# Attention and a gated unit on one core: new delays and slack in a list scheduler, bf16 norm sums, a shift turned in f16, and eight pairs' outputs turned by TensorE

## The chip, the core and the metric

The kernel runs on one core of one Trainium2 chip. The core has TensorE (PE: matmuls, with its weight loads told apart as PEld), VectorE (DVE), ScalarE (ACT), GpSimd (POOL) and SyncE (SP), which issues all of this kernel's DMAs. Each engine works through its own queue in order; semaphores tie the queues together. The metric is the device time of one execution in microseconds, given as a median over runs. A profile is one more execution with every instruction recorded. All times below are from such runs and profiles.

## The reference

Attention over 8 batches and 8 heads of 64, with 576 pooled queries and 1152 keys, followed by a unit with a spatial gate over the joined heads.

```python
q_pool = q.reshape(B, H, S // 2, 2, D).mean(axis=3)
scores = scale * np.matmul(q_pool, k.transpose(0, 1, 3, 2))
scores = scores - np.max(scores, axis=-1, keepdims=True)
attn = np.exp(scores)
attn = attn / (np.sum(attn, axis=-1, keepdims=True) + 1e-09)
x = np.matmul(attn, v)            # heads joined: (8, 576, 512)
...
h = np.maximum(x @ w_in, 0.0)     # 512 -> 1024
u, v = h[..., :512], h[..., 512:]
v_n = (v - mean) / np.sqrt(var + 1e-06)
v_s = np.einsum('ts,bsd->btd', w_spatial, v_n) + b_spatial
out = (u * v_s) @ w_out           # float32
```

## The kernel before

**Precision.** Nearly every f32 operand is split into a head and a rest in 16 bits (hi and lo), scaled by a power of two that `scales` (L340) finds: a matmul with a matrix of ones sums squares over the partitions, and three small VectorE instructions make two factors of the exponent.

**Pairs.** Two heads make a pair: 8 batches of 4 pairs, 32 in all. For each pair:

- `prep` (L535) scales and splits q and k and copies the parts to where the matmuls want them (DMAs).
- `maxima` (L594) computes the scores a first time, heads only, in 27 blocks of 128 x 384, into a PSUM tile named `pm` (or, while no gated unit is open, alternately `pw`). VectorE reduces each block to its row maxima (`mt`, L623).
- `shift` (L631) makes of the maxima two rows of f16 that are appended to q (`X`), so that the second product comes out with the maximum subtracted already. It is called twice a pair, for 5 and for 4 groups of 128 rows. It reduces `mt` to `mx`, turns `mx` by TensorE (L639, f32), works on the turned row in PSUM (L642), writes head and rest (L645, L646) and sends them by two DMAs (L649).
- `attention` (L792) computes the scores again in 18 blocks of 128 keys x 512 queries (`main_tile`: two matmuls each, L800 and L801, into one of three banks `pss`), takes the exponential on ScalarE into `pt` (L806, eight buffers), and splits `pt` on GpSimd (L826) into a bf16 top and an f16 rest. `values` (L700) multiplies both with v (L714, L720, L725). 64 further queries of each head go by `tail_tile` and `tail_values`.
- `values` ends each head with a division into `xm`. `turn_main` (L740) then splits the pair's 128 x 512 result into head and rest (`xc`: L746 on ScalarE; L747 on VectorE for the first eight pairs, on GpSimd after) and turns both by two DMA transposes (L750) into `xg`.

The maxima of pair i+1, the preparation of pair i+2, the values of pair i+1 and the weights (in the first eight pairs, `load_weights`, L401, with its `from_double`) are woven into the attention of pair i.

**Gated units.** Two batches make a unit (`gated_unit`, L846): some 580 matmuls of up to 512 columns through the banks `pw`. The first opens after the eighth pair, and four run in all, woven into the attention of later pairs. The last runs mostly alone.

**Order.** The program is written in a plausible order, and `Order.pin` (L183) then replaces each engine's order by that of a list schedule. `cost` (L146) gives each instruction two times: how long it holds its engine and when its result is there. `edges` (L101) gives the dependences, and the order in which buffers of a ring may be begun. The loop of `pin` always takes the engine that can start earliest and, on it, the instruction that is first in the program among those that are due. The order found is fixed by dependences that hold no semaphore. For the VectorE and GpSimd instructions that take two operands from SBUF (`two_from_sbuf`, L178) the schedule keeps them from overlapping. For loads it keeps a count of the DMA queue's backlog, `wire`.

```python
                at = {n: max(due[n], wire - 1000) if n in load else due[n] for n in ns}
                t = max(free[e], min(at.values()))
                n = min(n for n in ns if at[n] <= t)
...
            if shared[n]:
                if e == "DVE":
                    if t >= held[0]:
                        t = max(t, held[1] - 130)
```

## Time and profile before

| what | value |
|---|---|
| median of 3 runs | 1229.48 us (1221.91, 1229.48, 1231.46) |
| the profiled execution | 1221.1 us, of which the recorded span is 1219.0 us |
| mean granted TensorE clock | 0.98 of full speed |
| DMA traffic | 135.09 MB, mean 111 GB/s |
| issues of the DMA transposes of `turn_main` | 64, two a pair |
| matmuls of `scales` (f32, two instructions a call) | 48 calls |

Engine rows of the profile give busy time, share of the span and a count. A group's row names line, engine, operation, tiles written and read, shapes and count, then busy time with the mean of one in ns, then the engine's idle time just before them with what ended it. A row of waits reads: the engine and line that waited, what ended the wait, total us, times, longest. A matmul's time in a row includes its passage through the array, so the pace of matmuls is read from one start to the next; the same holds for VectorE's instructions. Stages are written as windows in us from the start of the span.

### The profile page before, as it was taken

The numbers are of one execution on the slowest core, as the hardware profiler recorded it, in microseconds if no ns is written. First come the engines' busy times: TensorE is split into PE (matmuls) and PEld (weight loads), VectorE is DVE, ScalarE is ACT, GpSimd is POOL, SyncE is SP. The second block draws the span as 40 slices with busy tenths as digits, with TensorE's granted clock in tenths as the row PEclk, the third lists the DMA queues.
The fourth block names the chain that finished last, engine by engine and source line by source line (L and its number), as shares of the span: only waits on it lengthen the run. The fifth ranks groups of instructions, "written<-read, shape, count | busy, mean of one in ns | idle before, by whom it ended". The sixth has DMA issues, their size and how long they took to land.

```text
span 1219.0 us, 34011 instructions
## 1 busy us (share of the span) xinstructions
PE 1143.2 (94%) x13504; PEld 712.6 (58%) x13504; DVE 897.0 (74%) x2163; ACT 890.6 (73%) x1659; POOL 909.6 (75%) x774
## 2 busy tenths in 40 slices
PE   3888888879999999999999999999999999999998
PEld 1555555556666666666666666666665666665453
DVE  5699999997889676865679777865669866841644
ACT  4788778678977887878777887878776786754423
POOL 2769998699888897888787887888887787874000
PEclk9989899899999999999999999999999999999999
DMA  5456464346443553266433443256343421121002
GB/s 189 162 169 169 118 196 120 112 126 169 122 123 95 122 142 105 49 167 179 117 80 99 140 118 89 63 145 196 93 115 98 106 76 47 39 53 45 1 1 78
DMA packets 97151, 135.09 MB, mean 111 GB/s; under 512 B 48544, under 2 KB 56736, under 8 KB 96480
## 3 DMA queue, kind: packets, MB, share of 16 engines
q1 hardware_dynamic: 96992, 132.92, 39.7%
q8 instruction: 106, 1.74, 0.6%
q14 instruction: 53, 0.43, 0.1%
HBM read 81.20 MB, written 9.44 MB: 74 GB/s over the span
## 4 chain that ended last, share of the span: by engine, by line
PE 72%; DVE 16%; ACT 3%; issue 1%; DMA 0%; ACTq 0%; DVEq 0%
PE pss L800 8%; PE pss L801 8%; PE pm L617 7%; PE pw L988 7%; PE pw L883 6%; DVE mt L623 6%; PE pw L1031 5%; PE pw L947 5%; PE o L725 4%; PE o L714 4%; PE o L720 4%; DVE vv L372 2%; PE pss L883 1%; PE pss L988 1%; PE pss L1031 1%
## 5 line engine op out<-in xcount | busy, mean ns | idle before, releaser
L826 POOL TENSOR_TENSOR pt<-pt 128x512 f16<-128x512 f32 x576 | 643.0, 1136 | 154.5 <-ACT pt L806 152.7
L806 ACT ACTIVATE pt<-pss,esc 128x512 f32<-128x512 f32 x576 | 386.7, 686 | 166.3 <-PE pss L801 104.0
L623 DVE TENSOR_REDUCE mt<-pm 128x1 f32<-128x384 f32 x733 | 387.9, 549 | 75.2 <-PE pm L617 66.4
L800 PE MATMUL pss<-qhi,khi 128*128 128x512 f16 x576 | 221.3, 385 | 18.3 <-ACT pt L806 16.9
L801 PE MATMUL pss<-xq,klo 66*128 66x512 f16 x576 | 221.3, 387 | 0.7 <-DMA xq<-mr 0.5
L617 PE MATMUL pm<-khi,qhi 128*128 128x384 f16 x655 | 208.6, 332 | 10.4 <-DVE mt L623 5.2
L714 PE MATMUL o<-vp,pt 128*128 128x65 f16 x2304 | 171.0, 194 | 0.4
L725 PE MATMUL o<-vp,pt 128*128 128x65 f16 x2304 | 169.7, 194 | 0.6 <-POOL pt L826 0.5
L714 PEld LDWEIGHTS <-pt 128*128 128x128 bf16 x2304 | 130.1, 99 | 67.1 <-issue 5.0
L720 PE MATMUL o<-vp,pt 128*128 128x64 f16 x2304 | 168.7, 194 | 0.0
L725 PEld LDWEIGHTS <-pt 128*128 128x128 f16 x2304 | 124.0, 99 | 32.0 <-issue 4.5
L617 PEld LDWEIGHTS <-qhi 128*128 128x128 f16 x768 | 75.3, 100 | 76.5 <-issue 30.2
L720 PEld LDWEIGHTS <-pt 128*128 128x128 bf16 x2304 | 112.2, 99 | 3.3 <-issue 0.3
L883 PE MATMUL pw<-wi_h,xg 128*128 128x512 f16 x240 | 88.4, 378 | 0.0
L801 PEld LDWEIGHTS <-klo 66*128 66x128 f16 x576 | 56.6, 99 | 51.8 <-issue 27.3
L826 POOL TENSOR_TENSOR ptl<-ptl 128x1152 f16<-128x1152 f32 x32 | 74.3, 2321 | 14.4 <-ACT ptl L822 14.4
L947 PE MATMUL pw<-xg,wi_h 128*128 128x512 f16 (+1 forms) x336 | 83.4, 325 | 0.0
L822 ACT ACTIVATE ptl<-pss,esc 128x256 f32<-128x256 f32 (+1 forms) x128 | 63.7, 497 | 26.4 <-PE pss L817 26.2
L988 PE MATMUL pw<-ws_h,vv 128*128 128x512 f16 x216 | 80.6, 379 | 0.0
L1031 PE MATMUL pw<-wo_h,vv 128*128 128x512 f16 x216 | 79.0, 378 | 1.1 <-DVE vv L372 0.9
L623 DVE TENSOR_REDUCE mt<-pw 128x1 f32<-128x384 f32 x131 | 69.6, 543 | 9.3 <-PE pw L617 8.9
L800 PEld LDWEIGHTS <-khi 128*128 128x128 f16 x576 | 57.0, 99 | 26.2 <-issue 6.8
(195 smaller groups left out, 2432.0 us busy)
## 6 DMA issues: line engine op xcount, KB each, us to landing
vt<-in_v_dram SPq DMA_DIRECT2D x56, 576.0 KB
qt<-in_qT_dram SPq DMA_DIRECT2D x32, 576.0 KB
kt<-in_kT_dram SPq DMA_DIRECT2D x32, 576.0 KB
khi<-kn SPq DMA_DIRECT2D x128, 144.0 KB
out_dram<-row SPq DMA_DIRECT2D x24, 256.0 KB
qhi<-xq SPq DMA_DIRECT2D x64, 72.0 KB
klo<-klo SPq DMA_DIRECT2D x32, 144.0 KB
vv<-in_w_in_dram SPq DMA_DIRECT2D x4, 1024.0 KB
```

Source lines behind the costliest of these rows:

```text
L617: nc.tensor.matmul(pm[:, :W], lhsT=qhl[:, h, c0 : c0 + P], rhs=khh[:, h, n * NB : (n + 1) * NB, :], start=True, stop=True,)
L623: nc.vector.reduce_max(out=mt[:, t, n : n + 1], in_=pm[:, :W], axis=AX.X)
L714: nc.tensor.matmul(o[:, t], lhsT=top[:, cols], rhs=vp[:, D : D + D1], start=c == 0 and t == 0, stop=False, skip_group_check=True,)
L720: nc.tensor.matmul(o[:, t, 0:D], lhsT=top[:, cols], rhs=vp[:, 0:D], start=False, stop=False, skip_group_check=True)
L725: nc.tensor.matmul(o[:, t], lhsT=rst[:, cols], rhs=vp[:, D : D + D1], start=False, stop=c == NC - 1, skip_group_check=True,)
L800: nc.tensor.matmul(o, lhsT=khh[:, h, c, :], rhs=qhl[:, h, q], start=True, stop=False)
L801: nc.tensor.matmul(o, lhsT=KL[0:KR, h, c, :], rhs=X[0:KR, h, q], start=False, stop=True)
L806: nc.scalar.activation(pt, ps, AF.Exp, bias=0.0, scale=esc)
L826: nc.gpsimd.tensor_sub(t.bitcast(F16)[..., 0::2], t, t.bitcast(BF16)[..., 1::2])
L883: nc.tensor.matmul(ph, lhsT=xa[:, cc, c0 : c0 + P], rhs=wa[:, cc, DH:DF], start=n == 0, stop=n == 3 * NCC - 1,)
L988: nc.tensor.matmul(pv, lhsT=l, rhs=r[:, 0:MAIN], **fl)
L1031: nc.tensor.matmul(py, lhsT=ga[:, fc, c0 : c0 + P], rhs=wa[:, fc, :], start=m == 0, stop=m == end - 1)
```

## The change

The diff has four parts, shown with the lines around them cut.

**The schedule's model.** The time from one engine's result to another engine's start, a constant 54 (140 ns towards GpSimd), becomes a table with 52 as the default. A second table, `SLACK`, adds to the time at which a TensorE instruction counts as due (not to when it could start, which is kept in `there`): 2100 ns behind GpSimd, 300 behind ScalarE and VectorE, 500 behind a DMA. A VectorE instruction with two SBUF operands is not picked while GpSimd holds such an operation, if another can start. Several constants of `cost` change, a DMA transpose's issue time among them.

```diff
+    DELAY = {("PE", "Activation"): 114, ("Activation", "Pool"): 77}
+    SLACK = {("Pool", "PE"): 2100, ("Activation", "PE"): 300, ("DVE", "PE"): 300, ("SP", "PE"): 500}
...
-            return 500, 2400 + big / 230
+            return (1230 if "Transpose" in ins.opcode else 560), 2400 + big / (100 if "Transpose" in ins.opcode else 230)
...
-            t = 0.84 * n + (175 if psum else 200) + 90 * min(flat, 2)
+            t = 0.84 * n + (157 if psum else 188) + 85 * (min(flat, 2) or (n == 1 and wide > 1))
             if len(ins.outs) > 1:
-                t += 90
+                return t - 10, t + 95
+            return t - 105, t
...
-            t = {F32: 2.1, F16: 2.0, BF16: 1.74}[xs[1].dtype] * n + 190
-        return t - 80, t
+            t = {F32: 2.1, F16: 2.0, BF16: 1.74}[xs[1].dtype] * n + 150
+            return t - 42, t
+        return t - 84, t
...
                     at = {n: max(due[n], wire - 1000) if n in load else due[n] for n in ns}
+                    if e == "DVE":
+                        for n in ns:
+                            if shared[n] and max(free[e], at[n]) >= held[0]:
+                                at[n] = max(at[n], held[1] - 130)
...
             own, out = cost[n]
+            t = max(free[e], there[n])
...
-                end = wire + 1900
+                end = wire + 1700
...
                 elif lane[m] != e:
-                    x = end + (140 if lane[m] == "Pool" else 54)
+                    x = end + self.DELAY.get((e, lane[m]), 52)
                 else:
-                    x = t if e == "PE" else end
-                due[m] = max(due[m], x)
+                    x = t if e == "PE" else end + 34
+                there[m] = max(there[m], x)
+                due[m] = max(due[m], x + (self.SLACK.get((e, lane[m]), 0) if through else 0))
```

**The norm sums.** `ones` becomes bf16, and the sums of squares are read as their upper halves, so the matmul is of 16-bit operands. The sums lose their lower bits; the factors come from the exponent alone.

```diff
-    ones = const.tile([P, P], F32, name="ones")
+    ident_h = const.tile([P, P], F16, name="ident_h")
+    nc.vector.tensor_copy(out=ident_h, in_=ident)
+    ones = const.tile([P, P], BF16, name="ones")
...
-        nc.tensor.matmul(pt[:, :n], lhsT=ones, rhs=sq, start=True, stop=True)
+        nc.tensor.matmul(pt[:, :n], lhsT=ones, rhs=sq.bitcast(BF16)[:, 1::2], start=True, stop=True)
```

**The shift.** The arithmetic is done before the turn, on 128 x 5 or 128 x 4 values in the free columns of the last maxima bank, and head and rest are turned together in f16 into the same bank. One copy then takes them to SBUF. No bank of its own is taken.

```diff
-        mx = sm.tile([P, NT], F32, name="mx", bufs=2)
-        nc.vector.reduce_max(out=mx[:, :n], in_=mt[:, a:z], axis=AX.X)
-        yield
-        yield
-        pt = ps_m.tile([P, 512], F32, name="pm")
-        nc.tensor.transpose(out=pt[:n, :P], in_=mx[:, :n], identity=ident)
-        mr = sm.tile([NT, 2, P], F16, name="mr", bufs=2)
-        m = pt[:n, :P]
-        nc.vector.tensor_scalar(
-            out=m, in0=m, scalar1=st["lnp"][:n], scalar2=1.0 / MROW, op0=ALU.subtract, op1=ALU.mult
-        )
-        nc.vector.tensor_copy(out=mr[:n, 0], in_=m)
-        nc.vector.tensor_sub(mr[:n, 1], m, mr[:n, 0])
+        m = pm[:, KEYS // 3 : KEYS // 3 + n]
+        nc.vector.reduce_max(out=m, in_=mt[:, a:z], axis=AX.X)
+        nc.vector.tensor_scalar(out=m, in0=m, scalar1=st["lnp"], scalar2=1.0 / MROW, op0=ALU.subtract, op1=ALU.mult)
+        mc = sm.tile([P, 2 * NT], F16, name="mc", bufs=2)
+        nc.vector.tensor_copy(out=mc[:, 0:n], in_=m)
+        nc.vector.tensor_sub(mc[:, n : 2 * n], m, mc[:, 0:n])
+        yield
+        yield
+        t = pm.bitcast(F16)[: 2 * n, 2 * (512 - P // 2) :]
+        nc.tensor.transpose(out=t, in_=mc[:, : 2 * n], identity=ident_h)
+        mr = sm.tile([2 * NT, P], F16, name="mr", bufs=2)
+        nc.vector.tensor_copy(out=mr[: 2 * n], in_=t)
...
-            nc.sync.dma_start(out=rows[:, a * P : z * P], in_=mr[:n, r])
+            nc.sync.dma_start(out=rows[:, a * P : z * P], in_=mr[r * n : (r + 1) * n])
```

**The first eight pairs' outputs.** `EARLY` is 8, the number that stood in the code at three places. For those pairs TensorE turns `xm` itself, in f32, in four transposes into one `pm` bank, and `x_split` (L685) makes head and rest from PSUM, straight into `xg`. For the others the old way stays, as `turn_by_dma`.

```diff
+        if i < EARLY:
+            ps = ps_m.tile([P, 512], F32, name="pm")
+            for t in range(4):
+                nc.tensor.transpose(out=ps[:, t * P : (t + 1) * P], in_=xm[:, t], identity=ident)
+            m0 = 0 if e == 0 else MAIN + P
+            x_split(n, hp, slice(m0, m0 + MAIN), ps)
+        else:
+            turn_by_dma(xm, n, e, hp)
...
         xc = wk.tile([P, 2, 4, P], F16, name="xc", bufs=1)
         nc.scalar.activation(xc[:, 0], xm, AF.Copy, bias=0.0, scale=1.0)
-        (nc.vector if i < 8 else nc.gpsimd).tensor_sub(xc[:, 1], xm, xc[:, 0])
+        nc.gpsimd.tensor_sub(xc[:, 1], xm, xc[:, 0])
```

More of the change, by code (lines that the diff above doesn't have):

```diff
@@ L210, in pin @@
         due = [0.0] * len(prog)
+        there = [0.0] * len(prog)
         free = dict.fromkeys(self.LANES, 0.0)
@@ L282, in attn_sgu_kernel @@
     WS_STEPS = 2
+    EARLY = 2 * NHP
     MOE_RATE = 0.5
@@ L517, in split_v @@
             hd = vp[:, h, :, D : 2 * D]
-            if i < 8:
+            if i < EARLY:
                 head(hd, vt[:, h], s_v)
@@ L572, in prep @@
         for a, z in ((0, 5), (5, NC)):
-            if i < 8:
+            if i < EARLY:
                 head(kn[:, a:z], k0[:, a:z], s_k)
@@ L626, in maxima, with shift @@
             if t == 4:
-                yield from shift(st, mt, 0, 5)
+                yield from shift(st, mt, pm, 0, 5)
         yield
-        yield from shift(st, mt, 5, NT)
-    def shift(st, mt, a, z):
+        yield from shift(st, mt, pm, 5, NT)
+    def shift(st, mt, pm, a, z):
         X = st["X"]
         n = z - a
-        mx = sm.tile([P, NT], F32, name="mx", bufs=2)
-        nc.vector.reduce_max(out=mx[:, :n], in_=mt[:, a:z], axis=AX.X)
+        m = pm[:, KEYS // 3 : KEYS // 3 + n]
[4 more added lines that the diff above has]
+        nc.vector.tensor_sub(mc[:, n : 2 * n], m, mc[:, 0:n])
         yield
         yield
-        pt = ps_m.tile([P, 512], F32, name="pm")
-        nc.tensor.transpose(out=pt[:n, :P], in_=mx[:, :n], identity=ident)
-        mr = sm.tile([NT, 2, P], F16, name="mr", bufs=2)
-        m = pt[:n, :P]
-        nc.vector.tensor_scalar(
-            out=m, in0=m, scalar1=st["lnp"][:n], scalar2=1.0 / MROW, op0=ALU.subtract, op1=ALU.mult
-        )
-        nc.vector.tensor_copy(out=mr[:n, 0], in_=m)
-        nc.vector.tensor_sub(mr[:n, 1], m, mr[:n, 0])
+        t = pm.bitcast(F16)[: 2 * n, 2 * (512 - P // 2) :]
+        nc.tensor.transpose(out=t, in_=mc[:, : 2 * n], identity=ident_h)
+        mr = sm.tile([2 * NT, P], F16, name="mr", bufs=2)
+        nc.vector.tensor_copy(out=mr[: 2 * n], in_=t)
         for r in range(2):
             rows = X[D + r : D + r + 1].rearrange("p h s -> p (h s)")
-            nc.sync.dma_start(out=rows[:, a * P : z * P], in_=mr[:n, r])
+            nc.sync.dma_start(out=rows[:, a * P : z * P], in_=mr[r * n : (r + 1) * n])
         yield
@@ L738, in values, with turn_by_dma @@
                 later.append([2, lambda: turn_main(i)])
-    def turn_main(i):
-        b, hp = divmod(i, NHP)
-        n, e = divmod(b, 2)
-        xm = state.pop(i)["xm"]
+    def turn_by_dma(xm, n, e, hp):
         xc = wk.tile([P, 2, 4, P], F16, name="xc", bufs=1)
         nc.scalar.activation(xc[:, 0], xm, AF.Copy, bias=0.0, scale=1.0)
-        (nc.vector if i < 8 else nc.gpsimd).tensor_sub(xc[:, 1], xm, xc[:, 0])
+        nc.gpsimd.tensor_sub(xc[:, 1], xm, xc[:, 0])
         m0 = 0 if e == 0 else MAIN + P
@@ L753, in turn_main @@
             )
+    def turn_main(i):
+        b, hp = divmod(i, NHP)
+        n, e = divmod(b, 2)
+        xm = state.pop(i)["xm"]
+        if i < EARLY:
+            ps = ps_m.tile([P, 512], F32, name="pm")
[5 more added lines that the diff above has]
+            turn_by_dma(xm, n, e, hp)
         if hp == NHP - 1:
```

## The prediction

> **What bounds the kernel now.** I read the page's first lines, then the busy time by windows, the waits and the chain in the stages so found, and last the groups of the lines that the diff touches.
>
> ```profile
> span 1219.0 us, 34011 instructions
> PE 1143.2 (94%) x13504; PEld 712.6 (58%) x13504; DVE 897.0 (74%) x2163; ACT 890.6 (73%) x1659; POOL 909.6 (75%) x774
> ...
> 0.00:30.00 30.00, 10.21 (x36) 4.11 (x37) 17.34 (x42) 13.21 (x28) 7.58 (x16) 0.93 0.58 192
> 30.00:285.00 255.00, 211.82 (x2750) 138.06 (x2749) 229.54 (x501) 195.58 (x358) 213.53 (x163) 0.91 0.52 146
> 285.00:1110.00 825.00, 816.52 (x10046) 518.30 (x10044) 599.34 (x1503) 641.87 (x1200) 683.16 (x591) 1.00 0.40 108
> 1110.00:1219.00 109.00, 104.69 (x682) 52.15 (x677) 50.80 (x120) 39.90 (x76) 5.33 (x5) 0.99 0.09 30
> ```
>
> The window rows give length, then busy us of PE, PEld, DVE, ACT and POOL, then the clock. The 94% is a mean over two regimes. From 285 us on, where gated units feed TensorE, it is busy in 816.5 of 825 us at full clock: there only less TensorE work or fewer gaps count. From 30 to 285 us (the first eight pairs) TensorE has 43 us idle, VectorE 25, GpSimd 41: a loop in which VectorE is the fullest, with GpSimd behind it. Since the units wait for pair eight, a microsecond saved there is a microsecond of the end.
>
> The waits from 30 to 285 us, and three pieces of the chain:
>
> ```profile
> POOL pt L826 <- ACT pt L806: 36.4, 13, 10.2
> ACT pt L806 <- PE o L725: 31.8, 15, 5.8
> DVE pm L642 <- PE pm L639: 4.8, 4, 2.1
> ...
> 106.96 5.62 DMA xq<-mr
> 140.93 3.25 DVE mt L623 x7
> 167.46 1.10 PE pm L757 x8
> ```
>
> GpSimd starves at pair borders and ScalarE then waits for buffers. 3.25 us for seven reduces is 464 ns a piece, though each shows 549 below: VectorE's instructions overlap by some 80 ns, which I take off every VectorE duration.
>
> **The change part by part.** Groups of the touched lines:
>
> ```profile
> L639 PE MATMUL pm<-ident,mx 128*5 128x128 f32 (+1 forms) x46 | 12.5, 272 | 0.0
> L345 PE MATMUL pm<-sq,ones 128*128 128x2 f32 x44 | 7.0, 228 | 0.0
> ...
> L345 PE MATMUL pm<-vt,ones 128*128 128x1 f32 x10 | 1.4, 209 | 0.0
> ...
> L345 PE MATMUL pm<-gt,ones 128*128 128x1 f32 x6 | 0.8, 208 | 0.0
> L345 PE MATMUL pm<-wst,ones 128*128 128x1 f32 x2 | 0.3, 210 | 0.0
> ...
> L623 DVE TENSOR_REDUCE mt<-pm 128x1 f32<-128x384 f32 x733 | 387.9, 549 | 75.2 <-PE pm L617 66.4 <-PE pm L608 3.6
> L642 DVE TENSOR_SCALAR pm<-pm,lnp 5x128 f32<-5x128 f32 x64 | 22.0, 344 | 55.2 <-PE pm L639 55.0
> L646 DVE TENSOR_TENSOR mr<-pm,mr 5x128 f16<-5x128 f32 x64 | 17.5, 274 | 1.2
> L645 DVE CAST mr<-pm 5x128 f16<-5x128 f32 x64 | 17.5, 273 | 0.9
> L355 DVE TENSOR_SCALAR qkr<-pm 128x2 int32<-128x2 int32 x32 | 4.9, 154 | 0.7
> L688 DVE TENSOR_TENSOR xg<-pm,xg 128x256 f16<-128x256 f32 x8 | 3.3, 415 | 0.1
> ```
> ```profile
> 301.94 0.29 PE L725 MATMUL o<-vp,pt 128*128 128x65 f16 x4
> ...
> 302.06 0.36 PE L345 MATMUL pm<-sq,ones 128*128 128x2 f32 x2
> ...
> 302.28 0.32 PE L608 MATMUL pm<-kn,qd 128*128 128x384 f16 x1
> ...
> 374.89 0.22 PE L947 MATMUL pw<-xg,wi_h 128*128 128x128 f16 x1
> 374.94 0.27 PE L639 MATMUL pm<-ident,mx 128*5 128x128 f32 x1
> 375.05 0.33 PE L617 MATMUL pm<-khi,qhi 128*128 128x384 f16 x1
> ```
>
> The matmul groups are those of 285 to 1110 us, the VectorE groups those of the whole run.
>
> *Norm sums.* A call holds TensorE from 302.06 to 302.28, 0.22 us for two f32 passes. One 16-bit pass over two columns is nearest to L725, four from 301.94 to 302.06, 0.03 each. That saves 0.19. In the bound stage stand 44 + 10 + 6 + 2 instructions, 31 calls: 5.9 us. Earlier calls hide under VectorE.
>
> *The turn in the shift.* L639 holds TensorE for 0.11 us (374.94 to 375.05). The f16 matmul of 128 columns before it takes 0.05. 46 turns in the stage save 0.06 each: 2.8, taken as 2.5. Norm sums and turns together: 8.4 us, bounds 6 and 9. This is the sure part.
>
> *VectorE in the shift.* Now 344 + 273 + 274, each less 80: 0.65 us a call. After it: three instructions on 128 x 5, priced by L355 at 154 less 80, and one copy of 128 values a row, priced by L645 at 193: 0.42. Twice a pair saves 0.46, over eight pairs 3.7 us. VectorE still stands before its last copy until TensorE has turned; behind it are the next reduces. That wait was 4.8 us in this stage, so 0 is taken, within plus or minus 4.8. The bank now stays in use from reduce to copy, but the old form took one for the turn and its three instructions: one of two is blocked either way. Beyond 285 us the saved VectorE time is worth nothing by itself.
>
> *Outputs of eight pairs.* The rows of what goes, and of what is slowed by GpSimd:
>
> ```profile
> L747 DVE TENSOR_TENSOR xc<-xm,xc x8: 668/1118/2243, 67.5 to 298.0; 128x512 f16<-128x512 f32 x8
> L372 DVE SCALAR_TENSOR_TENSOR vp<-vt,vs,vp x8: 809/1328/1686, 160.5 to 251.9; 128x576 f16<-128x576 f32 x8
> L372 DVE SCALAR_TENSOR_TENSOR qhi<-qt,qks,xq x9: 796/1070/1242, 39.1 to 271.3; 128x576 f16<-128x576 f32 x9
> L394 DVE SCALAR_TENSOR_TENSOR vv<-vv x6: 1203/2063/2657, 72.4 to 260.0; 128x1024 int32<-128x1024 int32 x6
> L396 DVE TENSOR_TENSOR u<-u,vv x6: 1216/1626/1981, 73.8 to 267.3; 128x1024 f32<-128x1024 f32 x6
> L826 POOL TENSOR_TENSOR pt<-pt x576: 1032/1043/2273, 33.4 to 1114.4; 128x512 f16<-128x512 f32 x192
> ...
> L746 ACT ACTIVATE xc<-xm 128x512 f16<-128x512 f32 x32 | 20.1, 628 | 5.2 <-DVE xm L733 4.6
> L750 SPq DMA_TRANSPOSE xg<-xc x64: 1188/1227/2377, 68.9 to 1119.5; - x64
> ```
>
> The subtraction at L747 has a median of 1.12 us. From PSUM a 256-wide one takes 415 ns and a reduce of 384 takes 549, so about 1.05 ns a column more: 512 columns, 0.68. Saved 0.4 a pair, 3.3 over eight. ScalarE's copy of the same 512 columns now reads PSUM; it stays near its 628 ns (bounds 0 and 0.1 more), covered by its 59 us idle in the stage. SP loses sixteen transposes of 1.23 us and the waits before them; behind them stood the small DMAs of the shift. TensorE gains 32 f32 transposes: eight of L757 take 1.10, so 0.14 each at most, 0.55 a pair, 4.4 us, on idle TensorE time; without that cover they cost 4.4. The extra bank is held for some 2 us a pair while three others still feed reduces of 0.46: 0, at worst the 2 us, 16 in all.
>
> *The schedule.* (a) VectorE avoids GpSimd. Median less minimum, times the count, over the four slowed groups that stay (L372 twice, L394, L396) is 4.2 + 2.5 + 5.2 + 2.5 = 14 us, and GpSimd's own stretch comes on top of it. The gain lies between 0 and 14; the list plans phases that the chip keeps only in part, so I take 7; the other sign, -7, is possible by the same rows. (b) The new constants barely move GpSimd's pace (1081 - 80 before, 1041 - 42 after, for a split whose median is 1043): 0. SP's transposes are now modelled at what L750 shows, so DMAs behind them are placed later. The 5.6 us of `xq<-mr` could shrink or recur: 0, plus or minus 5. (c) The slack lets TensorE prefer work whose inputs are long there. In the bound stage at most the 8.5 us of idle time can go; half, 4 us. At worst as much is added.
>
> *Sum.* VectorE's 3.7 + 3.3 + 7 = 14 us count at 0.7, since GpSimd and the pair borders also pace the first stage: 10. With 8.4 and 4 it is 22.4 us off. From the profiled execution's 1221.1 us that makes 1198.7. That execution is the fastest of the four shown (1221.1, 1221.9, 1229.5, 1231.5; mean 1226.0) and lies 8.4 below the median, so the forecast of a median starts from the mean: 1226.0 - 22.4 = 1203.6, forecast 1204.
>
> **What the skill adds.** The stretches (1203 to 2657, 1032 to 2273) are about one whole operation of the other engine. The Trainium skill, "SBUF — State Buffer", section "Who interferes with whom", says that the issue order decides which engine blocks, and that it blocks fully. The trace agrees. If the chip does not keep the planned phases, term (a) is 0 by that rule and the sum 1209. If it keeps them all, 1199.
>
> **The rivals.**
>
> *The first stage does not shorten (chance 0.18).* GpSimd is busy in 213.5 of 255 us, and borders starve it by 36.4. If these set the pace, VectorE's savings turn into waits, and 8.4 us remains: 1217.6, within 1%.
>
> *The port stalls nearly vanish (0.12).* Then GpSimd is freed as well: 7 + 14 + 8.4 + 8.5 = 38, with some 8 of border waits, 1180.
>
> *Held buffers (0.07), slower.* The slack puts the `values` matmuls up to 2.1 us later in the first stage, `pt` comes free later, and `ACT pt L806 <- PE o L725` grows. If all its 15 waits grow by 2.1, 31.5 us are added while only 8.4 + 4 are saved: 1245. It needs 8 of the 15 to come back to the median of before, and 14 to be slower by 1%. Against it: TensorE idles there, eight buffers of 1.04 us of GpSimd's work each cover far more than 2.1 us, and the slack doesn't delay a start where nothing else is due.
>
> *A slower clock in the first stage (0.05).* Two rows:
>
> ```profile
> 90.00:120.00 30.00, 25.02 (x351) 15.91 (x349) 28.07 (x61) 24.75 (x48) 28.71 (x21) 1.00 0.65 173
> 210.00:240.00 30.00, 25.25 (x314) 16.04 (x314) 29.31 (x56) 18.11 (x32) 23.10 (x18) 0.85 0.43 122
> ```
>
> At 0.85, 30 us hold 314 matmuls where full clock holds 351. If the stage fell from 0.91 to 0.85, 15 us of TensorE time are lost, a third of it on the path: 1209. The Trainium skill, "TensorE: Matmul & The Clock Gate", section "Part 4: PE-mode transpose", says that transposes don't count as activity for the clock, which would push this way. No row here shows it.
>
> **How the numbers follow.** The likeliest case has 0.58 and its own range 1192 to 1216. The low end, 1184, takes in most of the vanished stalls. The high end, 1226, takes in the unshortened stage with the runs' spread; beyond both lie about 2 in 10. A run of this kernel tells about 1% from no change: faster means below 1217, slower above 1242. Faster: 0.54 + 0.12 + 0.04 + 0.03 = 0.73. Slower: 0.07. Within: 0.20.
>
> **What would show it.** Right: VectorE's waits at the shift's copy no longer than L642's, no VectorE subtraction with GpSimd stretch in `turn_main`, first gated matmul 8 to 12 us earlier than 285, L345 at one instruction a call, TensorE idle in the bound stage below 8.5 us. Wrong: the first stage as long as now, ScalarE's waits for L725 well above 31.8 us, or new TensorE gaps after 285 us.

## The result, and the profile after

| | median | lowest to highest | runs |
|---|---|---|---|
| before, same chip and session | 1224.82 us | 1220.59 to 1231.46 | 8 |
| after | 1233.9 us | 1231.72 to 1238.67 | 8 |

The ratio after to before is 1.0086, with a 95% interval of 1.006 to 1.0112. The change costs about 10 us, just inside the 1% that the prediction called no change. A gain of 22 us had been forecast: the kernel became slower where it was to become faster.

The first lines of the page of after; the profiled execution took 1231.81 us:

```profile
span 1229.9 us, 33935 instructions
PE 1146.7 (93%) x13488; PEld 705.8 (57%) x13488; DVE 894.4 (73%) x2228; ACT 889.4 (72%) x1659; POOL 904.0 (73%) x774
```

The busy time by windows of after, in the same four stages as before (window, length, busy us of PE, PEld, DVE, ACT and POOL with counts, clock, DMA share, GB/s):

```profile
0.00:30.00 30.00, 10.65 (x35) 3.67 (x36) 17.66 (x45) 13.35 (x29) 7.64 (x16) 0.91 0.58 193
30.00:285.00 255.00, 207.90 (x2686) 136.11 (x2685) 227.15 (x500) 193.43 (x349) 207.47 (x160) 0.90 0.46 137
285.00:1110.00 825.00, 812.11 (x9949) 506.57 (x9948) 597.08 (x1557) 636.95 (x1199) 675.69 (x587) 1.00 0.40 107
1110.00:1230.00 120.00, 116.08 (x827) 59.44 (x823) 52.52 (x127) 45.66 (x84) 13.15 (x13) 1.00 0.10 32
```

Read the second and third rows against those of before. In 255 us of the first stage TensorE does 2686 matmuls where it did 2750, at nearly the same clock (0.90, before 0.91), and every other engine is less busy too: they wait more on one another. In the bound stage TensorE was idle for 8.5 us and is now idle for 12.9. The first row of a gated matmul says when that stage begins:

```profile
L908 PE MATMUL pw<-wi_h,xg x240: 376/379/390, 291.4 to 1143.7; 128*128 128x512 f16 x120
```

That is 291.4 us, where before it was 285.0. Busy time hides small gaps, since a matmul's record includes its passage through the array. So I also counted from starts: each matmul form has a usual distance from one start to the next (its pace). The turn of the shift is counted at the pace of an f16 matmul of the same 128 columns with full-width weights, 0.06 us. The sum of the paces is called work, and what is left of the time is called lost. For one profiled execution each:

| kernel | span | first gated matmul | work, lost ahead of it | work, lost from there on |
|---|---|---|---|---|
| before | 1219.0 | 285.0 | 177.1, 107.9 | 900.9, 33.2 |
| after | 1229.9 | 291.4 | 177.6, 113.8 | 892.9, 45.6 |

So after = before + 6.4 (first stage) - 8.0 (work) + 12.4 (lost) = +10.8 us. The work fell by about what the prediction called the sure part, 8.4; but for the turn (2.5 of it) that is so by the way of counting, and whatever the turn costs beyond 0.06 us stands in the lost time. Two things have to be found: what makes the first stage longer, and what TensorE loses in the bound stage.

The waits of after from 30 to 285 us (the engine and line that waited, what ended the wait, total us, times, longest), and behind them the one of before at the same turn:

```profile
POOL pt L851 <- ACT pt L831: 43.4, 19, 9.5
ACT pt L831 <- PE o L739: 23.0, 18, 2.6
PEld L658 <- DVE mc L654: 15.8, 12, 2.7
...
PE pw L658 <- DVE mc L654: 7.6, 5, 2.5
...
DVE mr L660 <- PE pw L658: 3.5, 4, 2.1
```
```profile
PE pm L639 <- DVE mx L635: 2.2, 3, 1.1
```

TensorE's matmuls stand 7.6 us before the shift's turn (L658) until VectorE has made head and rest (`mc`, L654). Before, they stood 2.2 us there. The row of PEld, 15.8 us, holds the same waits as the weight loads see them, in part while earlier matmuls still run, so the two aren't added. VectorE's own wait for the turned row, 3.5 us, is no longer than L642's was (4.8). So VectorE comes late to a place where TensorE, and all the maxima behind the turn, wait for it. It is one place of several: over the stage, 34.5 us of TensorE's idle time end with a result of VectorE, where before it was 21.6.

The timeline of after at such a place (start, duration, instruction, idle time before it and what ended that):

```profile
181.66 1.04 POOL L851 TENSOR_TENSOR pt<-pt 128x512 f16<-128x512 f32 x1
...
181.67 1.65 DVE L386 SCALAR_TENSOR_TENSOR vp<-vt,vs,vp 128x576 f16<-128x576 f32 x1
...
182.66 1.56 POOL L851 TENSOR_TENSOR pt<-pt 128x512 f16<-128x512 f32 x1
...
184.18 1.04 POOL L851 TENSOR_TENSOR pt<-pt 128x512 f16<-128x512 f32 x1
...
184.18 1.65 DVE L386 SCALAR_TENSOR_TENSOR vp<-vt,vs,vp 128x576 f16<-128x576 f32 x1
...
185.75 0.15 DVE L653 CAST mc<-pw 128x5 f16<-128x5 f32 x1
...
186.29 0.15 DVE L654 TENSOR_TENSOR mc<-pw,mc 128x5 f16<-128x5 f32 x1
...
186.49 0.22 PE L658 MATMUL pw<-ident_h,mc 128*10 128x128 f16 x1 [1.40 <-DVE mc L654]
```

GpSimd begins a split at 181.66. VectorE's two-operand instruction comes 0.01 us later, and takes 1.65 us where its shortest takes 0.80. GpSimd's next split, begun while VectorE worked, takes 1.56 for 1.04. The second `vp` comes within the same hundredth as the split after that, 184.18, and takes 1.65 again. Both stand ahead of the shift's `mc` in VectorE's queue, and TensorE idles for 1.40 us.

The second place, in the timeline of after in the bound stage:

```profile
600.35 0.28 PE L734 MATMUL o<-vp,pt 128*128 128x64 f16 x4
...
600.56 0.08 PEld L658 LDWEIGHTS <-mc 128*8 128x8 f16 x1
600.56 0.22 PE L658 MATMUL pm<-ident_h,mc 128*8 128x128 f16 x1
600.71 0.10 PEld L825 LDWEIGHTS <-khi 128*128 128x128 f16 x1
600.71 0.39 PE L825 MATMUL pss<-qhi,khi 128*128 128x512 f16 x1
```

The four L734 pace at 0.03 us and leave TensorE at 600.47. The turn starts at 600.56 with its weights, and the next matmul, again with its weights, at 600.71. The turn thus holds TensorE for 0.25 us (0.09 + 0.15), where the prediction had 0.05. Nothing is said to wait here: the weights of the turn, 8 columns wide, are not loaded ahead, and neither are those behind it.

### The profile page after: what moved, and what is told of

Read it like the earlier page. It is cut to its first block, busy times and chain, and to the rows that moved or that the text cites. A ratio compares the mean times of both kernels' runs of the same rounds, so it can differ in the third digit from the quotient of the medians.

```text
span 1229.9 us, 33935 instructions
## 1 busy us (share of the span) xinstructions
PE 1146.7 (93%) x13488; PEld 705.8 (57%) x13488; DVE 894.4 (73%) x2228; ACT 889.4 (72%) x1659; POOL 904.0 (73%) x774
## 4 chain that ended last, share of the span: by engine, by line
PE 71%; DVE 22%; ACT 2%; issue 2%; DMA 1%; SPq 1%; POOL 0%; DVEq 0%; ACTq 0%; POOLq 0%
DVE mt L637 8%; PE pss L825 8%; PE pss L826 7%; PE pm L631 7%; PE pw L1013 7%; PE pw L908 6%; PE pw L1056 5%; PE pw L972 4%; PE o L728 4%; PE o L739 4%; PE o L734 4%; DVE vv L386 2%; DVE vp L386 1%; PE pss L908 1%; DVE qhi L386 1%
## 5 line engine op out<-in xcount | busy, mean ns | idle before, releaser
L826 PE MATMUL pss<-xq,klo 66*128 66x512 f16 x576 | 222.5, 388 | 0.0
L631 PE MATMUL pm<-khi,qhi 128*128 128x384 f16 x655 | 203.7, 331 | 15.1 <-DVE mt L637 11.3
L734 PE MATMUL o<-vp,pt 128*128 128x64 f16 x2304 | 167.6, 194 | 0.0
L739 PEld LDWEIGHTS <-pt 128*128 128x128 f16 x2304 | 131.0, 99 | 59.4 <-issue 3.6
L728 PEld LDWEIGHTS <-pt 128*128 128x128 bf16 x2304 | 125.5, 99 | 58.2 <-DVE xm L747 7.2
L734 PEld LDWEIGHTS <-pt 128*128 128x128 bf16 x2304 | 112.1, 98 | 3.0
L826 PEld LDWEIGHTS <-klo 66*128 66x128 f16 x576 | 56.4, 98 | 43.7 <-issue 18.5
L637 DVE TENSOR_REDUCE mt<-pw 128x1 f32<-128x384 f32 x131 | 69.2, 546 | 14.8 <-PE pw L631 14.4
L851 POOL TENSOR_TENSOR ptl<-ptl 128x1152 f16<-128x1152 f32 x32 | 71.2, 2224 | 8.3 <-ACT ptl L847 8.1
L825 PEld LDWEIGHTS <-khi 128*128 128x128 f16 x576 | 56.7, 99 | 33.9 <-issue 12.4
```

Of the source, the lines that this page charges most:

```text
L631: nc.tensor.matmul(pm[:, :W], lhsT=qhl[:, h, c0 : c0 + P], rhs=khh[:, h, n * NB : (n + 1) * NB, :], start=True, stop=True,)
L637: nc.vector.reduce_max(out=mt[:, t, n : n + 1], in_=pm[:, :W], axis=AX.X)
L728: nc.tensor.matmul(o[:, t], lhsT=top[:, cols], rhs=vp[:, D : D + D1], start=c == 0 and t == 0, stop=False, skip_group_check=True,)
L734: nc.tensor.matmul(o[:, t, 0:D], lhsT=top[:, cols], rhs=vp[:, 0:D], start=False, stop=False, skip_group_check=True)
L739: nc.tensor.matmul(o[:, t], lhsT=rst[:, cols], rhs=vp[:, D : D + D1], start=False, stop=c == NC - 1, skip_group_check=True,)
L825: nc.tensor.matmul(o, lhsT=khh[:, h, c, :], rhs=qhl[:, h, q], start=True, stop=False)
```

## The experiments

Two suspicions to begin with: the schedule's choice by which VectorE avoids GpSimd (rival: its new constants, its slack, or the program's new shape), and the f16 turn (rivals: the transpose mode, or the width of its weights). Each ratio is to runs of the kernel before on the same chip.

| kernel | ratio | 95% interval | median, us |
|---|---|---|---|
| a_norms | 0.9987 | 0.9954 to 1.0021 | 1220.0 |
| b_shift | 1.0042 | 1.0018 to 1.0066 | 1230.08 |
| c_early | 0.9988 | 0.9963 to 1.0013 | 1221.42 |
| d_order | 1.0026 | 0.9996 to 1.0057 | 1228.76 |
| e_mmturn | 1.0104 | 1.0066 to 1.0142 | 1234.88 |
| f_shift_mm | 1.0053 | 1.0031 to 1.0075 | 1229.22 |
| g_oldorder | 0.9961 | 0.9935 to 0.9986 | 1219.37 |
| h_noslack | 1.0103 | 1.0065 to 1.014 | 1235.93 |
| j_pad | 0.9901 | 0.9877 to 0.9925 | 1208.74 |
| k_noavoid | 0.9962 | 0.9942 to 0.9982 | 1214.39 |
| l_avoidonly | 1.0179 | 1.0148 to 1.0211 | 1243.23 |
| m_consts | 0.9953 | 0.9933 to 0.9973 | 1215.48 |
| n_both | 0.9859 | 0.9831 to 0.9887 | 1206.35 |
| p_sooner | 0.9966 | 0.9944 to 0.9988 | 1218.8 |
| q_shiftpad | 0.9953 | 0.9926 to 0.998 | 1217.81 |
| t_oldshift | 0.9927 | 0.9902 to 0.9953 | 1214.65 |

### Each part by itself

a_norms, b_shift and c_early put one part of the program into the kernel before, and d_order puts the new `Order` alone; g_oldorder is after with the `Order` of before.

```diff
a_norms, on before
+    ones = const.tile([P, P], BF16, name="ones")
+        nc.tensor.matmul(pt[:, :n], lhsT=ones, rhs=sq.bitcast(BF16)[:, 1::2], start=True, stop=True)
b_shift, on before: the new shift()
c_early, on before: the new turn_main()
d_order, on before: the new class Order
g_oldorder, on after: the class Order of before
```

Expected of a_norms:

> The kernel before with the bf16 norm sums alone; its order is found anew by the old schedule. Theory T (the f16 turn of the shift costs TensorE more than the f32 one and eats the gain of the norm sums): the sums are a clean gain, some 31 calls of 0.15 to 0.19 us in the stage that TensorE bounds, so 5 to 6 us faster than before, ratio about 0.995. Theory S (the new schedule model is what costs): the same here, since the schedule is the old one. If instead any new order costs by chance, the ratio lies anywhere between 0.99 and 1.01.

Of b_shift:

> The kernel before with the new shift alone. Theory T: in the trace of after the f16 turn shows 0.09 us of empty TensorE before it and 0.15 us from its start to the next matmul, 0.25 in all, where the f32 turn takes 0.11; 46 turns in the bound stage cost 6 us more, against up to 4 us that VectorE saves in the first stage: ratio 1.000 to 1.006. My prediction's own reading (a turn of 0.05 us): 0.995. Theory S: as the prediction, about 0.995.

Of c_early:

> The kernel before with the outputs of the first eight pairs turned by TensorE, all else old. Theory E (in the first stage TensorE and ScalarE stand in order before these turns, while they wait for VectorE's xm): the first stage grows by 3 to 6 us, ratio 1.003 to 1.005. The prediction: about 3 us shorter, 0.997. Theories T and S expect no loss here.

Of d_order:

> The kernel before with the new schedule model alone (delays, slack, costs, the choice that avoids GpSimd). Theory S: this is the loss, ratio 1.008 or more. Theory T: no loss, 0.995 to 1.002, and no f16 turn in it. The prediction: 0.991 (7 us of port stalls at 0.7 and 4 us of TensorE gaps).

Of g_oldorder:

> The changed kernel's program under the old schedule model. Theory T (the turn is the main loss, the schedule a small one): 1.002 to 1.006. Theory S (the schedule is the main loss): 0.996 to 1.001. The three program parts measured alone add to 1.0017.

Measured: by itself the shift costs 0.42%, and the norms, the outputs and the order each lie within their error of nothing. The whole program under the old order gains 0.39%, and under the new one it loses 0.86%: with this program the new order costs 1.2%, though with the old one its cost isn't clear (1.0026). By starts, a_norms has 5.6 us less work from the first gated matmul on (895.3 for 900.9), and c_early reaches that matmul 5.4 us sooner (279.6). So the work and the first stage change as was said, but neither shows clearly in the time. In c_early's profile the time from the first gated matmul to the end is longer by 4.9 us (938.9 for 934.0), which takes back nearly all of the 5.4. The loss of b_shift lies in the first stage: its first gated matmul comes at 292.8, 7.8 us later than before, and from there to the end it takes 933.9 us. a_norms stayed short of its expected 0.995, and d_order lies between the ranges of its two theories.

### The turn: the mode or the width

e_mmturn turns by an ordinary matmul into f32 instead of by a transpose, in after; f_shift_mm does so in b_shift. j_pad keeps the transpose and gives it weights of 128 columns, of which those beyond head and rest are zero; it stands on g_oldorder.

```diff
e_mmturn, on after (f_shift_mm: the same on b_shift)
-        t = pm.bitcast(F16)[: 2 * n, 2 * (512 - P // 2) :]
-        nc.tensor.transpose(out=t, in_=mc[:, : 2 * n], identity=ident_h)
+        t = pm[: 2 * n, KEYS // 3 :]
+        nc.tensor.matmul(t, lhsT=mc[:, : 2 * n], rhs=ident_h, start=True, stop=True)
j_pad, on g_oldorder
+    mcs = [const.tile([P, P], F16, name=f"mc{i}") for i in range(2)]
+    for t in mcs:
+        nc.vector.memset(t, 0.0)
...
-        mc = sm.tile([P, 2 * NT], F16, name="mc", bufs=2)
+        mc = mcs[a > 0]
...
-        t = pm.bitcast(F16)[: 2 * n, 2 * (512 - P // 2) :]
-        nc.tensor.transpose(out=t, in_=mc[:, : 2 * n], identity=ident_h)
+        t = pm.bitcast(F16)[:, 2 * (512 - P // 2) :]
+        nc.tensor.transpose(out=t, in_=mc, identity=ident_h)
...
-        nc.vector.tensor_copy(out=mr[: 2 * n], in_=t)
+        nc.vector.tensor_copy(out=mr[: 2 * n], in_=t[: 2 * n])
```

Expected of e_mmturn:

> The changed kernel with its f16 turn written as an ordinary matmul with the identity into f32 PSUM (the copy that follows then converts). Theory T: the empty stretches around the turn vanish, 0.25 us falls to about 0.06, 46 turns give 8 to 9 us in the stage that TensorE bounds: ratio to the kernel before 1.000 to 1.003 where the change had 1.0086, and in the trace the next matmul starts 0.06 us after the turn. Rival R (the turn stands still because its input comes late, the drain is a wait in disguise): the ratio stays near 1.008 and the gaps stay.

Of f_shift_mm:

> The kernel before with the new shift alone, its turn as an ordinary matmul. The new shift with the f16 turn had 1.0042. Theory T: 8 to 9 us less than that, 0.995 to 0.998. Rival W (the shift loses in the first stage, because TensorE stands before the turn until VectorE has done four instructions and not one): it stays above 1.000, with the first gated matmul as late as in the run with the f16 turn, 293 us against 285 before.

Of j_pad:

> The changed program under the old schedule (0.9961), with the turn's weights padded by zero columns from 8 or 10 to 128, so that it is a full-width 16-bit matmul like the others. Theory N (the 0.19 us of empty TensorE around each turn come from its narrow 16-bit weights, which are not loaded ahead; the ordinary matmul with the same weights had the same gaps): the turn costs 0.06 us, 46 turns give back some 8 us in the bound stage, ratio 0.988 to 0.991. Rival M (any change of the weights' element type or of the identity operand drains it): the gaps stay, 0.995 to 0.998.

Measured: the ordinary matmul is no better (1.0104 beside 1.0086, and 1.0053 beside 1.0042). f_shift_mm also keeps the late gated unit of b_shift (293.3), as rival W had it. The timeline of e_mmturn:

```profile
406.09 0.22 PE L658 MATMUL pm<-ident_h,mc 128*8 128x128 f16 x1 [0.67 <-DVE mc L654]
...
406.24 0.39 PE L825 MATMUL pss<-qhi,khi 128*128 128x512 f16 x1
```

The 0.15 us behind the turn is there again, so the theory that the transpose mode empties TensorE falls. The width is left, and padding to 128 columns brings 0.9961 to 0.9901, 0.6% with intervals apart. The same instruction in n_both (below), which has the padding too:

```profile
509.22 0.38 PE L825 MATMUL pss<-qhi,khi 128*128 128x512 f16 x1
509.23 0.10 PEld L658 LDWEIGHTS <-mc 128*128 128x128 f16 x1
509.44 0.22 PE L658 MATMUL pm<-ident_h,mc 128*128 128x128 f16 x1
...
509.50 0.38 PE L826 MATMUL pss<-xq,klo 66*128 66x512 f16 x1
```

Now the weights are loaded at 509.23, under the matmul before, and the turn holds TensorE for 0.06 us. Against 0.25 that is 0.19 us for each of 46 turns, 8.7 us of the 12.4 that after loses in the bound stage. The two pairs of profiles that differ by the padding alone, and by the order found anew for it, fit this: from the first gated matmul to the end j_pad takes 925.8 us where g_oldorder takes 933.7, and n_both 920.8 where k_noavoid takes 928.7, 7.9 us less in both. The width as such isn't the whole condition: the old f32 turn had weights of 5 columns and took 0.11 us without such gaps.

### The schedule: choice, slack, constants

h_noslack empties the slack in after. k_noavoid takes only the choice out of after, l_avoidonly puts only the choice into g_oldorder, and m_consts is k_noavoid without the slack. p_sooner keeps the choice but lets VectorE's instruction be picked 600 ns before GpSimd's operation ends in the plan. The time at which the plan then starts it stays 130 ns before that end.

```diff
h_noslack, on after (m_consts: the same on k_noavoid)
+    SLACK = {}
k_noavoid, on after (l_avoidonly: adds these lines to g_oldorder)
-                    if e == "DVE":
-                        for n in ns:
-                            if shared[n] and max(free[e], at[n]) >= held[0]:
-                                at[n] = max(at[n], held[1] - 130)
p_sooner, on after
-                                at[n] = max(at[n], held[1] - 130)
+                                at[n] = max(at[n], held[1] - 600)
```

Expected of h_noslack:

> The changed kernel with an empty slack table, the rest of the new schedule model kept. If the slack is what makes the new order worse (TensorE stood 23 us before the turns in the first stage, 7 us with the old model): 1.003 to 1.006. If the delays, the costs or the choice that avoids GpSimd do it: 1.008 as it was. If the slack helps: 1.010 or more.

Of k_noavoid:

> The changed kernel without the choice that keeps VectorE's two-operand instructions from GpSimd; slack, delays and costs are the new ones. Theory A (that choice is what makes the new schedule worse: it puts off the preparation of the next pairs behind reduces while port stalls did not fall, 31.7 us after against 29.9 before): 0.995 to 1.000, first gated matmul back at 285 us. Theory C (the new delays and costs do it): 1.007 to 1.010 as it was.

Of l_avoidonly:

> The changed program under the old schedule model plus the choice that avoids GpSimd alone. Theory A: 1.004 to 1.009, first gated matmul at 290 us or later. Theory C: 0.994 to 0.998, as the old schedule gave.

Of m_consts:

> The changed program under the new delays and costs alone: no slack, and no choice that avoids GpSimd. Theory A: 0.995 to 1.000. Theory C: 1.007 to 1.011. If it comes out between, both have a part.

Of p_sooner:

> The changed kernel with the avoiding choice kept, but VectorE's two-operand instructions become pickable 600 ns before GpSimd's operation ends in the plan, not 130. Theory P (on the chip VectorE reaches them just after GpSimd has begun its next operation, so it waits for a whole one: in the trace of after, where GpSimd is running at their start, 0.94 us of its operation is left in the median, 0.67 without the choice): coming sooner they get the port first, 0.996 to 1.001. Rival Q (what costs is that the preparation is put off behind reduces): the choice still puts it off, 1.005 to 1.010.

Measured: without the choice 1.0086 becomes 0.9962, and with it alone 0.9961 becomes 1.0179. It is the choice, in both directions and with intervals far apart; alone it costs more than the 1.004 to 1.009 that had been expected. The slack does nothing that can be seen, with the choice (1.0103 beside 1.0086) or without (0.9962 beside 0.9953), and delays and costs alone do no harm (m_consts 0.9953 beside g_oldorder 0.9961).

The first and the bound stage by windows, of k_noavoid, then of g_oldorder, then of l_avoidonly (g_oldorder with the choice):

```profile
30.00:285.00 255.00, 215.57 (x2832) 138.92 (x2832) 227.31 (x524) 201.85 (x369) 220.82 (x170) 0.94 0.47 143
285.00:1110.00 825.00, 817.93 (x10034) 512.96 (x10032) 591.27 (x1542) 631.07 (x1193) 674.92 (x588) 1.00 0.39 106
```
```profile
30.00:285.00 255.00, 213.71 (x2803) 139.03 (x2803) 224.49 (x523) 199.65 (x365) 217.40 (x166) 0.93 0.48 141
285.00:1110.00 825.00, 815.88 (x9968) 510.59 (x9968) 584.11 (x1543) 637.23 (x1191) 676.50 (x588) 1.00 0.39 107
```
```profile
30.00:285.00 255.00, 211.05 (x2712) 138.11 (x2711) 232.17 (x507) 194.03 (x351) 205.04 (x161) 0.89 0.46 138
285.00:1110.00 825.00, 801.69 (x9772) 501.57 (x9770) 602.23 (x1548) 635.27 (x1184) 667.27 (x578) 1.00 0.38 106
```

In the first stage VectorE is the busier one where less gets done: 232 us for 507 instructions in l_avoidonly, against 224 for 523 in g_oldorder. The bound stage suffers too: there TensorE idles for 23.3 us with the choice and for 9.1 without, and for 12.9 in after where k_noavoid, with the same narrow turn, idles for 7.1. The table has one profiled execution of each kernel, in us. "Until VectorE" is the idle time of TensorE's matmuls that ended with a result of VectorE, in the first and in the bound stage.

| kernel | the choice | first gated matmul | from it to the end | until VectorE |
|---|---|---|---|---|
| before | no | 285.0 | 934.0 | 21.6, 6.2 |
| d_order | yes | 288.8 | 937.2 | 40.4, 11.0 |
| g_oldorder | no | 285.0 | 933.7 | 21.2, 8.8 |
| l_avoidonly | yes | 288.5 | 953.0 | 34.8, 21.7 |
| k_noavoid | no | 283.0 | 928.7 | 23.0, 6.5 |
| after | yes | 291.4 | 938.5 | 34.5, 11.8 |
| m_consts | no | 287.2 | 933.8 | 22.4, 12.6 |
| h_noslack | yes | 288.8 | 947.0 | 36.9, 19.9 |
| p_sooner | picked at 600 ns | 284.6 | 930.4 | 26.2, 5.0 |

The kernels stand in pairs without and with the choice (d_order has the new constants and the slack as well). With it TensorE waits longer for VectorE in each pair and in both stages, and the loss isn't one of the first stage alone: of the 18.2 us between k_noavoid and after, 9.8 lie behind the first gated matmul, and of the 22.8 between g_oldorder and l_avoidonly, 19.3. (The profile of m_consts is the slowest of its twelve executions, 1222.82 us, where their median is 1215.48.)

The choice was to save VectorE from being stretched. The stretch is duration less the shortest of the form, summed over VectorE's two-operand instructions of the first stage. It is about 32 us in after, 35 in l_avoidonly and 30 in before, but 26 in k_noavoid and 24 in g_oldorder. It doesn't mark the choice by itself: a_norms and b_shift, which are without it, show 32 and 33 as well, and m_consts 33, of which 8 are in one instruction recorded with 9.08 us. GpSimd's own stretch goes the other way: 36 us in after and 32 in l_avoidonly, for 40 in k_noavoid and g_oldorder. The waits of k_noavoid before the turn (the matmuls' 7.6 us in after):

```profile
PEld L654 <- DVE mc L650: 8.2, 7, 2.5
PE pw L654 <- DVE mc L650: 5.4, 4, 2.4
```

This place is no measure of the choice either: the matmuls' wait there is 1.2 us in l_avoidonly and 1.3 in h_noslack, which both have the choice and are the slower for it. (The 23 us in the expectation of h_noslack is the sum of matmuls and weight loads, 7.6 + 15.8.)

The choice doesn't let VectorE meet the other engine less often: 44 of 60 two-operand instructions start while GpSimd is at work in after, 43 of 63 in k_noavoid. In the first stage it meets it at a worse moment. The median time that GpSimd then still needs is 0.94 us in after, 0.98 in l_avoidonly and in d_order, though 0.75 in h_noslack; without the choice it is 0.5 to 0.7, and one GpSimd operation takes 1.04. By the code, both schedules place such an instruction 130 ns ahead of GpSimd's end, and GpSimd's next operation behind it. Without the choice the plan lets VectorE stand until then; nothing on the chip holds it, so it starts whenever its inputs are there. With the choice other VectorE instructions fill that time, so it does come at about that moment. But no semaphore holds the order between the two queues either, and one that comes a little late finds the next GpSimd operation just begun and waits for most of it, as in the timeline at 181.67. p_sooner, with 600 for 130, loses nothing any more (0.9966, with 0.5 us left in the median), and gains nothing over k_noavoid's 0.9962. The two slowed groups of after, then of p_sooner, by source line from 30 to 285 us (shortest, median and longest ns, first and last start):

```profile
L386 DVE SCALAR_TENSOR_TENSOR vp<-vt,vs,vp x8: 803/1591/1955, 165.5 to 257.5; 128x576 f16<-128x576 f32 x8
L386 DVE SCALAR_TENSOR_TENSOR wi_l<-u,wis,wi_h x4: 1627/2024/2295, 198.0 to 213.4; 128x1024 f16<-128x1024 f32 x4
```
```profile
L386 DVE SCALAR_TENSOR_TENSOR vp<-vt,vs,vp x8: 810/1130/2183, 162.9 to 235.4; 128x576 f16<-128x576 f32 x8
L386 DVE SCALAR_TENSOR_TENSOR wi_l<-u,wis,wi_h x4: 1270/1302/1460, 187.3 to 197.3; 128x1024 f16<-128x1024 f32 x4
```

The medians fall from 1591 to 1130 and from 2024 to 1302 ns. p_sooner also puts fewer instructions off, so it can't tell "comes earlier" from "is put off less". In the first stage the phases speak for the first. In the bound stage they don't: there the time that is left is 0.55 us in after and 0.52 in k_noavoid, so that part of the loss needs another reason. That the choice puts VectorE's work off, and with it what TensorE waits for, would be one; no run shows it by itself.

### Both faults mended, and the parts once more

n_both is after without the choice and with the padded turn. q_shiftpad is b_shift with the padded turn. t_oldshift is before with the new norm sums and outputs but the old shift.

```diff
n_both: k_noavoid with the padding of j_pad
q_shiftpad: b_shift with the padding of j_pad
t_oldshift: before with the edits of a_norms and c_early
```

Expected of n_both:

> The changed kernel with both faults mended: no choice that avoids GpSimd (0.9962 alone) and the turn's weights padded to full width (0.6% in the old order). If the two add: 0.989 to 0.991. If the order found anew eats one of them: 0.993 to 0.997.

Of q_shiftpad:

> The kernel before with the new shift alone, its turn's weights padded to 128 columns. With narrow weights it had 1.0042. Theory N: 46 turns give back 8 us in the bound stage, 0.997 to 0.999. Rival W (the shift's own order in the first stage costs 8 us, first gated matmul at 293 us, and that stays): 1.002 or more, or a gain only in so far as the first stage shortens.

Of t_oldshift:

> The kernel before with the norm sums and the early outputs, its old shift and its old schedule. Alone they had 0.9987 and 0.9988. If parts add: 0.9975. The same with the new shift had 0.9961 (narrow) and 0.9901 (padded); if the new shift with padded weights is worth its 8 us, this one lies at 0.995 to 0.999.

Measured: n_both is 0.9859 (0.9831 to 0.9887), 1206.35 us, and beats both kernels, by more than the expected 0.989 to 0.991. Its busy time by windows:

```profile
30.00:285.00 255.00, 215.45 (x2830) 140.74 (x2829) 227.21 (x523) 200.84 (x368) 220.59 (x169) 0.93 0.47 142
285.00:1110.00 825.00, 817.82 (x10074) 515.77 (x10073) 593.65 (x1549) 632.65 (x1197) 676.90 (x590) 1.00 0.40 107
```

TensorE idles for 7.2 us in the bound stage and does 10074 matmuls there, where before did 10046. By starts, its span is 14.8 us shorter than that of before: 1.6 in the first stage, 10.3 of work and 3.0 of lost time.

The padding turns the shift alone from a cost (1.0042) into a gain (0.9953). t_oldshift gains 0.73%, more than was expected, though its two parts alone gained 0.13% and 0.12%. So half of n_both's gain is there without the new shift, and the padded new shift isn't shown to beat the old one: j_pad, the same with it, has 0.9901, and the intervals overlap. The parts don't add: every edit has the whole order found anew. In q_shiftpad's profile the first gated matmul comes only at 296.3 us, against 285.0 in before, while its runs are faster; that execution, 1226.83 us, is the slowest of twelve (their median is 1217.81), and what it shows of the others stays open.

## Why the prediction was wrong

*Norm sums, -5.9: right as TensorE's work.* The calls now stand in one instruction each, as expected. The source line from 285 to 1110 us:

```profile
L359 PE MATMUL pm<-sq,ones x22: 163/167/168, 309.6 to 1041.4; 128*128 128x2 bf16 x22
```

At a pace of 0.03 us a call, a_norms has 5.6 us less work from the first gated matmul on. In the time it isn't seen alone (0.9987, with 1 inside the interval).

*The turn in the shift, -2.5: the step that failed, with the wrong sign.* It priced the f16 turn at 0.05 us by L947, a matmul with 128 columns of f16 that has weights of 128 columns too. It looked at what passes through and not at the weights. At 0.25 us the turn costs 46 x 0.14 = 6.4 us more than the f32 one. Padded, it takes 0.06, near the forecast. "The sure part" held the second largest error.

*VectorE in the shift and outputs of eight pairs: the prices right, the gain in time not shown.* In the groups of after from 30 to 285 us, the subtraction from PSUM and the four turns:

```profile
L774 PE MATMUL pm<-ident,xm 128*128 128x128 f32 x28 | 5.4, 299 | 0.0
L702 DVE TENSOR_TENSOR xg<-pm,xg 128x512 f16<-128x512 f32 (+1 forms) x8 | 5.1, 647 | 0.4 <-ACT xg L701 0.4
```

The mean of 647 ns mixes in one 256-wide instruction of 415; the seven of 512 columns take 681 ns, forecast as 0.68 us. c_early reached the gated unit 5.4 us sooner and lost nearly all of that behind it, so "a microsecond saved there is a microsecond of the end" doesn't hold in its profile. TensorE didn't stand idle for the turns' inputs (0.0 us); whether their own time came out of idle time, the row doesn't say. The shift's VectorE instructions take 0.43 us a call (226 + 158 + 155 + 208 ns, each less 80), forecast as 0.42, but the forecast 3.7 us of the first stage didn't come: alone, the new shift reached the gated unit 7.8 us later. The shift's wait at its copy, 3.5 us, is within the bound that was set for it. What was missed is the opposite wait, TensorE's for VectorE: with the arithmetic ahead of the turn, TensorE's matmuls, which stood 2.2 us there before, stand 5.4 in k_noavoid and 4.2 in g_oldorder.

*VectorE avoids GpSimd, -7 (its term (a)): the step that cost most, and again the sign.* The prediction wrote "the other sign, -7, is possible by the same rows" and took the gain. The choice cost 1.2% in after, some 15 us by the ratios with and without it, where the sum had counted 0.7 x 7 = 5 us of gain. The step that failed was to read the choice as fewer stalls of VectorE and to count nothing for what its waiting does to TensorE: the stalls didn't shrink (some 32 us for 26 without the choice), and TensorE stood longer for VectorE's results, 34.5 us for 23.0 in the first stage and 11.8 for 6.5 in the bound stage. The Trainium skill, "SBUF — State Buffer", section "Who interferes with whom", says that the issue order decides which engine blocks. The trace agrees: at 181.67 GpSimd had issued first, and VectorE's instruction took 1.65 us for 0.80. The prediction drew from it that unkept phases would make the term 0. The term is a loss, and for the first stage the phases give a reason: the plan aims at the very moment when GpSimd begins again. That this is the whole reason isn't shown.

*New constants, 0: right* (m_consts beside g_oldorder). *Slack, -4: nothing measurable*, though TensorE's idle time in the bound stage is lower with it in both pairs of profiles (12.9 us in after for 20.7 in h_noslack, 7.1 in k_noavoid for 9.5 in m_consts).

*The rivals.* Held buffers: refuted, since ScalarE's waits for `values` fell from 31.8 us to 23.0, and taking the slack out gained nothing. Vanished stalls: refuted, since VectorE's stretch in the first stage is some 32 us for 30 before. A slower clock: 0.90 against 0.91, too small to explain the loss against before. But the changed program without the choice has 0.94 (k_noavoid) and 0.93 (g_oldorder), and whether the lower clock adds to the choice's cost or only follows from TensorE's waits, no run here tells. The first stage that doesn't shorten: nearest, but it got longer, for a reason that wasn't among the rivals; the loss by (a) stood as a bound of a term and got no chance of its own. Without (a) and the slack the sum of the prediction is 0.7 x 7 + 8.4 = 13.3 us; n_both, without (a) and with the turn at its forecast price, is 1.41% or 17 us faster than before, though by its profile more of that lies in the bound stage and less in the first than was forecast.

*What stays open.* How the 15 us of the choice divide between the stalls themselves, the work that is put off and the clock; and why the parts don't add. The remaining 3.7 us (12.4 - 8.7) that after loses in the bound stage go with the choice by the profiles, since k_noavoid, with the same turn, idles there for 7.1 us and not for 12.9.

## What to carry to other kernels

A list schedule can count on the order of two engines only where a semaphore keeps it. Here, at a resource that one engine holds alone, a plan that lets the other arrive at the moment of release was worse than none, so test such a plan as an experiment of its own, and look for its cost in every stage and at every engine that waits for the one it holds back. Price a small matmul by one with weights of the same width and type, and look at the starts around it, since no wait shows the gap; here filling narrow 16-bit weights up with zeros was worth 0.6% to 1%. Where the order is found anew for each program, measure the parts together as well as alone.

## What the runs showed of the hardware

An f16 matmul of 128 columns with weights of 8 or 10 columns leaves TensorE empty for about 0.09 us ahead of it (600.47 to 600.56) and about as long behind it, and so holds it for 0.25 us; with weights of 128 columns it holds it for 0.06 (509.44 to 509.50). Transpose or ordinary matmul makes no difference. The f32 turn with 5 columns (0.11 us) and the f16 weights of 66 rows and 128 columns (L826) show no such gap. Why the narrow 16-bit weights aren't loaded ahead, no run here shows.
